# Four interleaved attention layers on one core: earlier statistics and weight requests, later query factors

## The chip, the cores and the metric

The kernel runs on one core of a Trainium2 chip. The metric is the time of one execution on the device, in microseconds (us). A core has TensorE (PE, matmuls and transposes), VectorE (DVE), ScalarE (ACT), GpSimd (POOL) and SyncE (SP), which here does nothing but issue DMAs.

## The reference

Input x has S = 2048 rows of D = 512; there are H = 32 heads of 16. Four layers run in the order A, B, A, B, each as x + layer(layernorm(x)), both A layers with the same weights, both B layers too.

```python
def A(x):                                   # linear attention, learned feature map
    q, k, v = heads(x @ wqkv)
    pq, pk = q @ w_phi[h], k @ w_phi[h]
    phi = lambda p: concat(softmax(p), softmax(-p))       # 16 -> 32 features
    kv, z = phi(pk).T @ v, sum(phi(pk))
    return heads_back((phi(pq) @ kv) / (phi(pq) @ z + 1e-6)) @ wo

def B(x):                                   # four segments of 512 rows
    q, k, v = heads(x @ wq), heads(x @ wk), heads(x @ wv)
    for s in range(4):
        a_dot = softmax(q_s @ k_s.T / 4 + causal_mask) @ v_s
        a_mem = (elu1(q_s) @ M) / (elu1(q_s) @ z + 1e-6)  # M, z: segments before
        o_s = g * a_mem + (1 - g) * a_dot                 # g = sigmoid(beta)
        M, z = M + elu1(k_s).T @ v_s, z + sum(elu1(k_s))
    return heads_back(o) @ wo
```

## The kernel before

Rows are handled in 16 tiles of 128 rows by 512, in segments of four tiles. Between layers x lies in DRAM. All projections run as three matmuls on a high and a low part of each operand (`mm3`), so each transposed tile is made twice: ACT copies the high part out of PSUM (names `hh`, `oh`, `hi`), and DVE takes the difference as the low part (`hl`, `ol`, `lo`; `columns`, `turn` and `proj` do this). A low part inside `wait(...)` is put off by one slot where its table entry ends in "~".

**Order.** Python generators are interleaved step by step, and that order is written out by hand: `Ordered` wraps DVE, ACT, POOL and SP, and inside stretches with `ordered[0]` each engine keeps the program's order. `strict[0]` does the same for PE. SP issues nearly all DMAs in that order, and its issue of one DMA waits for the DMA eight before it.

**Layer A, pass 1** takes segments in the order `SEGS` = 1, 2, 3, 0. For the first layer `first()` writes the start out strictly: it loads the first rows and the raw weights, folds `w_phi` into the query and key weights, splits them into high and low parts, and makes the first v tiles. After it `norm_T` brings the next segment: four row loads into the pool tag `x` (four buffers), `bn_stats` per tile on DVE (`moments`), the root on ACT, the normalisation on ACT (`normal`), then transposes and high and low parts (`columns`). `prepare()` runs beside pass 1 and splits the weights of the later layers by way of DRAM.

**Layer A, pass 2** has 17 iterations, i = 0 to 16. One iteration transposes the query features `P` of tile i in two halves, applies `scale_q` to tile i+1 (sums `es`, reciprocal and factor `rr` on DVE, one product on POOL), turns the output of tile i-1 (`turn`: `oh`, `ol`), multiplies with `KN` in two halves (`weigh`), makes the differences of tile i+3 on POOL, asks for the queries of tile i+4 (`load_q`), projects tile i-1 with `wo` (`out_proj`), adds the residual row tile (tags `xr` and `ot`) and stores it. It then loads the next residual tile. One iteration has nine steps.

**The crossing into layer B.** The first `A20` = 76 steps of pass 2 run before layer B's `steps`. Into them `opening` is interleaved, one step every three from step 42 on. It calls `start()`, which makes two sets of the tiles Q and K (tag `e8`) and fills fixed rows of them by DMAs: mask rows into Q and K, and then ones into K over part of what the mask DMA wrote. Then it asks for the first four row tiles, makes their statistics, and at last asks for the value weights `bwv` (two halves of 1 MB) and for two tiles of `wqk` (0.5 MB each, `queue_w`).

**Layer B** runs slots k from -31 on; `BEFORE` says which projection, v tile or transposition falls into which slot before the first attention product. `maxima` and `attend` make the attention of 32 blocks m of four heads; `finish` transposes a block's result and `weigh`s it into the sums. From the second segment on, `weigh` multiplies on DVE and adds on POOL.

Names in the profile: line 162 is the wrapper of DVE, ACT, POOL and SP, line 184 `mm`, line 188 `tp` (transposes). The tile names carry the reading: `x` row tiles, `xr` and `ot` residual tiles, `g` the PSUM tiles of all projections and transposes, `e<-mask` and `e<-ones` the DMAs of `start()`.

## Time and profile before

| | |
|---|---|
| three runs, median | 1655.01 us |
| lowest and highest | 1649.2 and 1658.6 us |
| profiled execution, its own time | 1656.99 us |
| its span in the trace | 1655.3 us |
| its mean granted PE clock | 0.967 |
| DMA | 195.76 MB, mean 118 GB/s |

The profile is that of one execution. A row of the timeline gives start and duration in us, the engine, the line, the operation with output and input tiles, and in brackets the engine's idle time before it with what released it. A row of the waits gives engine, line and tile, what was waited for, then total us, number and longest. Several equal instructions in a row are one line with a count; the start is that of the first and the time is the engine's.

### The profile page before, as it was taken

To read this page: it belongs to the slowest core of one execution; us is meant where nothing else is said; L and a number is where in the kernel's file an instruction comes from. 1 tells how busy PE (TensorE), PEld (TensorE's weight loads), DVE (VectorE), ACT (ScalarE), POOL (GpSimd) and SP (SyncE) were. 2 spreads that over 40 slices of the span, in tenths; PEclk is the share of its full clock that TensorE was granted. 3 is DMA by queue.
4 is the path that set the end of the run, shared out by engine and by line. 5 is a ranking of instruction groups with operands and counts; after the bars stand their busy time and mean duration, and the time that the engine had idled before them with its cause. 6 is when DMAs were issued, how large, how long until landed. Compare 5 with 4: busy or idle time off the path is not lost.

```text
span 1655.3 us, 28153 instructions
## 1 busy us (share of the span) xinstructions
PE 1532.1 (93%) x9856; PEld 1094.4 (66%) x9856; DVE 1135.8 (69%) x3286; ACT 786.9 (48%) x1178; POOL 643.3 (39%) x972
## 2 busy tenths in 40 slices
PE   7799995998899999999999999788889999999998
PEld 6687884775566666666568888667655666666554
DVE  4575764376787877888655647536677778777783
ACT  4444333324656556556433333233355655654553
POOL 1366642222444354333222336323134445533422
PEclk9999997899999999999999999898999999999999
DMA  7348135434533533534242111454344445343331
GB/s 284 101 134 266 65 100 175 141 109 116 173 97 97 154 90 107 145 96 125 69 159 64 46 70 39 130 193 123 105 133 122 116 116 134 85 135 92 90 87 49
DMA packets 101124, 195.76 MB, mean 118 GB/s; under 512 B 13560, under 2 KB 27128, under 8 KB 97912
## 3 DMA queue, kind: packets, MB, share of 16 engines
q1 hardware_dynamic: 99832, 193.44, 39.2%
q8 instruction: 79, 1.29, 0.3%
q10 hardware_dynamic: 1152, 0.52, 0.1%
q14 instruction: 61, 0.50, 0.1%
HBM read 101.05 MB, written 39.85 MB: 85 GB/s over the span
## 4 chain that ended last, share of the span: by engine, by line
PE 71%; DVE 16%; issue 4%; ACT 4%; DMA 3%; POOL 2%; SPq 1%; ACTq 0%; DVEq 0%; POOLq 0%
PE g L184 43%; DVE mx L162 8%; PE mx L184 8%; PE lg L184 8%; PE pv L184 6%; PE g L188 6%; DVE mxs L162 2%; POOL P L162 1%; ACT tb L162 1%; ACT P L162 1%; DMA wqk<-wqk 1%; DVE es L162 1%; DVE ta L162 1%; DVE bs L162 1%; SPq L162 1%
## 5 line engine op out<-in xcount | busy, mean ns | idle before, releaser
L162 DVE CUSTOM_DVE_ANT_0 mx<-mx,mask 128x128 f32<-128x128 f32 (+3 forms) x1024 | 510.9, 499 | 185.2 <-PE mx L184 150.7
L162 ACT ACTIVATE P<-lg 128x1024 f32<-128x1024 f32 x320 | 328.8, 1028 | 186.8 <-PE lg L184 176.1
L162 POOL TENSOR_SCALAR_AFFINE_SELECT P<-P 128x256 f32<-128x256 f32 (+1 forms) x448 | 191.3, 442 | 445.5 <-ACT P L162 444.2
L184 PE MATMUL g<-hh,wqk 128*128 128x512 f32 x512 | 183.7, 413 | 16.4 <-DMA wqk<-wqk 15.9
L184 PE MATMUL g<-w,oh 128*128 128x512 f32 x512 | 177.4, 429 | 9.1 <-DVE ol L162 5.7
L184 PE MATMUL lg<-e,e 64*128 64x256 f32 (+2 forms) x1024 | 169.5, 389 | 8.1 <-ACT P L162 5.9
L184 PE MATMUL mx<-e,e 63*128 63x256 f32 (+2 forms) x1024 | 156.9, 363 | 21.4 <-DVE mxs L162 15.6
L184 PE MATMUL pv<-P,v 128*32 128x512 f32 (+3 forms) x2048 | 167.4, 446 | 0.0
L184 PEld LDWEIGHTS lg<-e,e 64*128 64x128 f32 x1024 | 81.7, 185 | 104.5 <-issue 55.1
L184 PE MATMUL g<-w,hh 128*128 128x512 f32 x448 | 146.6, 408 | 3.5 <-ACT tb L162 3.0
L162 DVE DVE_READ_ACCUMULATOR2_ANT mxs<- 128x1 f32 x1024 | 144.9, 141 | 0.0
L184 PEld LDWEIGHTS mx<-e,e 63*128 63x128 f32 x1024 | 83.8, 186 | 70.4 <-DVE mxs L162 49.9
L184 PEld LDWEIGHTS g<-hh,wqk 128*128 128x128 f32 x512 | 98.3, 192 | 38.5 <-issue 16.7
L184 PEld LDWEIGHTS pv<-P,v 128*32 128x32 f32 x2048 | 54.0, 110 | 100.2 <-issue 89.4
L184 PEld LDWEIGHTS g<-w,oh 128*128 128x128 f32 x512 | 94.0, 199 | 35.0 <-DVE ol L162 7.0
L162 POOL TENSOR_SCALAR tb<-tb 128x512 f32<-128x512 f32 x48 | 71.5, 1490 | 108.1 <-ACT tb L162 108.1
L184 PE MATMUL g<-w,ol 128*128 128x512 f32 x256 | 105.2, 412 | 1.1 <-DVE ol L162 1.1
L162 ACT CAST ta<-g 128x512 fp32r<-128x512 f32 x64 | 37.5, 586 | 136.1 <-PE g L184 136.0
L184 PE MATMUL g<-hl,wqk 128*128 128x512 f32 x256 | 101.7, 397 | 0.0
L184 PEld LDWEIGHTS g<-w,hh 128*128 128x128 f32 x448 | 80.6, 190 | 23.1 <-ACT tb L162 5.1
L162 POOL TENSOR_TENSOR P<-P,rr 128x512 f32<-128x512 f32 x32 | 33.9, 1060 | 151.2 <-DVE rr L162 151.2
L162 ACT COPY P<-g 128x512 f32<-128x512 f32 x64 | 34.7, 589 | 116.5 <-PE g L188 116.5
(132 smaller groups left out, 2781.8 us busy)
## 6 DMA issues: line engine op xcount, KB each, us to landing
e<-ta SPq DMA_DIRECT2D x384, 128.0 KB
wqk<-wqk SPq DMA_DIRECT2D x64, 512.0 KB
x<-x SPq DMA_DIRECT2D x48, 256.0 KB
xr<-in SPq DMA_DIRECT2D x28, 256.0 KB
pq<-tb SPq DMA_DIRECT2D x24, 256.0 KB
tb<-pq SPq DMA_DIRECT2D x24, 256.0 KB
x<-xr SPq DMA_DIRECT2D x24, 256.0 KB
xr<-x SPq DMA_DIRECT2D x24, 256.0 KB
```

What stands on the lines that cost most here:

```text
L162: i = f(*a, **k)
L184: return held(nc.tensor.matmul(*a, **k))
L188: return held(nc.tensor.transpose(*a))
```

## The change

- In `first()` the next segment's `norm_T` is created before the v weights are split, so its row loads are asked for there, and it is advanced 3, 2, 3 and 2 steps behind the four v tiles (`NEXT`), with its refinement on POOL. Pass 1 then goes on with what is left of it.
- `opening` begins at step 30 of pass 2, not 42: two `queue_w`, the two halves of `bwv`, one a step, then the rows, then `start()`, then the statistics.
- `start()` writes each Q and K tile's fixed rows once: `ones` has 32 rows, taken from a new column of `bd` (one in rows 15 and 31, zero elsewhere), so that no second DMA goes into K.
- `scale_q` of tile i+1 stands behind `turn`, not behind the transposes; that of the second tile of the last segment stands in pass 1 ahead of KN.
- Four entries of `BEFORE` lose their "~".
- For the last block of all, `weigh` adds on DVE and not on POOL.

```diff
+NEXT = (3, 2, 3, 2)
...
-BEFORE = {-30: "ln0", -29: "ln0", -28: "ln0", -27: "ln0", -25: "q0~", -23: "v0", -21: "k0~", -20: "load", -19: "v1",
-          -18: "n", -17: "v2 n", -16: "n", -15: "n n", -14: "q1~ n", -13: "n", -12: "v3 n", -11: "n", -10: "k1~ n",
+BEFORE = {-30: "ln0", -29: "ln0", -28: "ln0", -27: "ln0", -25: "q0", -23: "v0", -21: "k0", -20: "load", -19: "v1",
+          -18: "n", -17: "v2 n", -16: "n", -15: "n n", -14: "q1 n", -13: "n", -12: "v3 n", -11: "n", -10: "k1 n",
...
-        dve.memset(ones, 1.0)
+        dve.tensor_copy(ones, bd[0:32, 25:26].broadcast_to([32, P]))
...
             for t, k in zip((hi, lo), kept[key]):
                 dma(t, k)
+                yield
...
-    def weigh(out, p, eps, add):
+    def weigh(out, p, eps, add, eng=pool):
...
-        pool.tensor_tensor(out=out, in0=out, in1=t, op=ADD)
+        eng.tensor_tensor(out=out, in0=out, in1=t, op=ADD)
...
             next(kfold)
+            side = norm_T(self.xsrc, SEGS[1], nxt, "e8", slow=True, off=True)
+            next(side)
             for kc in range(NC):
...
                         next(qfold)
+                for _ in range(NEXT[t]):
+                    next(side)
...
-                    side = chain(norm_T(self.xsrc, SEGS[n + 1], hTs, spare), v_tile(hTs, wv, vv, ("g", G)))
+                    side = norm_T(self.xsrc, SEGS[n + 1], hTs, spare)
+                    if first and n == 0:
+                        hTs, side = nxt, ahead
+                    side = chain(side, v_tile(hTs, wv, vv, ("g", G)))
...
                     if t == 6:
+                        scale_q(e[5])
                         KN = self.KN = sp.tile([P, 8, 4, VW], F32, tag="KN", bufs=1, name=nm("KN"))
...
-                        if half == 1 and i + 1 < NT:
-                            scale_q(self.e[i + 1])
                         yield
                 if i > 0:
                     oT = turn([o[:, c * P : (c + 1) * P] for c in range(NC)])
+                    if i + 1 < NT:
+                        scale_q(self.e[i + 1])
...
-                for t in (Q, K):
-                    dma(t[3:P:4].rearrange("p a t -> p (a t)"),
-                        mask[0:32, 0:P].unsqueeze(1).broadcast_to([32, 16, P]))
-                dma(K[63:P:64].rearrange("p a t -> p (a t)"), ones[0:2, :].unsqueeze(1).broadcast_to([2, 16, P]))
+                for t, rows in ((Q, mask[0:32, 0:P]), (K, ones)):
+                    dma(t[3:P:4].rearrange("p a t -> p (a t)"), rows.unsqueeze(1).broadcast_to([32, 16, P]))
...
-                  pt.rearrange("p (q h e) -> p q h e", q=4, h=4), 0.0, s > 0)
+                  pt.rearrange("p (q h e) -> p q h e", q=4, h=4), 0.0, s > 0,
+                  dve if m == 8 * NSEG - 1 else pool)
...
             self.wnext = [(m, c) for _ in range(NSEG) for c in range(NC) for m in range(2)]
-            self.start()
-            self.norm0 = self.norm(0)
-            for _ in range(11):
-                next(self.norm0)
-                yield
-            self.wv = load_w("bwv")
             for _ in range(2):
                 self.queue_w()
+                yield
+            w = []
+            side = bring(w, "bwv")
+            self.wv = w
+            for _ in side:
+                yield
+            self.norm0 = self.norm(0)
+            next(self.norm0)
+            self.start()
+            for _ in range(10):
+                yield
+                next(self.norm0)
...
-            if k >= 42 and k % 3 == 0:
+            if k >= 30 and k % 3 == 0:
```

More of the change, by code (lines that the diff above doesn't have):

```diff
@@ L193, in interleave_kernel @@
     ident = cp.tile([P, P], F32, name="ident")
-    bd = cp.tile([P, 25], F32, name="bd")
+    bd = cp.tile([P, 26], F32, name="bd")
     bdA, bdB = bd[:, 0:8], bd[:, 8:16]
@@ L199, in interleave_kernel @@
     share = cp.tile([P, 8], F32, name="share")
-    ones = cp.tile([4, P], F32, name="ones")
+    ones = cp.tile([32, P], F32, name="ones")
     def constants():
@@ L568, in __init__, with first @@
             self.pqs, self.e, self.raw = {}, {}, {}
-        def first(self, hT, vv):
+        def first(self, hT, vv, nxt):
             ordered[0] = strict[0] = True
@@ L630, in first @@
             floor.update(ends)
-            return wq, wk, wv
+            return wq, wk, wv, side
         def pass1(self, first):
-            hTs, vv = [], []
+            hTs, vv, nxt = [], [], []
             if first:
-                wq, wk, wv = self.first(hTs, vv)
+                wq, wk, wv, ahead = self.first(hTs, vv, nxt)
             else:
@@ L1258 @@
     p = np.arange(P)
-    bd = np.zeros((P, 25), np.float32)
+    bd = np.zeros((P, 26), np.float32)
+    bd[[15, 31], 25] = 1.0
     bd[p, 24] = p % 32 < 16
```

## The prediction

> **What bounds the kernel now.** I read the page's first part first, because it tells which engine can set the time at all.

> ```profile
> span 1655.3 us, 28153 instructions
> PE 1532.1 (93%) x9856; PEld 1094.4 (66%) x9856; DVE 1135.8 (69%) x3286; ACT 786.9 (48%) x1178; POOL 643.3 (39%) x972
> ```

> PE is busy for 1532.1 of 1655.3 us, and the change removes no matmul. So no more than 1655.3 - 1532.1 = 123.2 us of idle time can be won, plus what PE lost by running at a lower clock. Next I read PE's own waits (total, times, longest, in us), because only a wait of PE is worth anything here.

> ```profile
> PE g L184 <- DVE xr L162: 18.5, 2, 9.7
> PE g L184 <- DMA wqk<-wqk: 15.9, 2, 8.1
> PE g L188 <- ACT x L162: 8.1, 1, 8.1
> PE g L184 <- DVE ol L162: 6.8, 6, 1.7
> PE g L188 <- ACT tb L162: 5.6, 2, 2.8
> PE g L188 <- POOL P L162: 3.5, 2, 1.8
> PE g L188 <- POOL tmp L162: 3.2, 2, 2.5
> ```

> These seven rows hold 61.6 us, and each edit aims at one or two of them. I took them one at a time, with the timeline around each. A fast measurement here spreads from 1649.2 to 1658.6 us, so about 0.5% (8 us) is what can be told from no change. The profiled execution took 1656.99 us: its span and 1.7 around it, 1.98 above the median 1655.01. All sums are made against 1656.99, and 1.98 is taken off at the end.

> **Second rows' statistics among the first weights.** The windows give us, PE busy (instructions), granted PE clock, DMA share, GB/s; the rows under them are PE's, SP's and DVE's in the same stretch.

> ```profile
> 41.00:49.00 8.00, 0.26 (x1) 0.77 0.36 148
> 49.00:59.00 10.00, 7.40 (x32) 0.84 0.38 106
> ...
> 37.05 0.62 PE L184 MATMUL g<-w,hh 128*128 128x512 f32 x2
> 49.91 7.21 SPq L162 DMA_DIRECT2D x<-in  x4
> 53.34 0.69 DVE L162 BATCH_NORM_STATS2 bs<-x 128x6 f32<-128x512 f32 x1 [0.86 <-DMA x<-in]
> 55.34 0.68 DVE L162 TENSOR_TENSOR e<-g,e 128x512 fp32r<-128x512 f32 x1
> 56.07 0.66 PE L188 MATMUL g<-ident,x 128*128 128x128 f32 x4 [1.91 <-DVE e L162]
> ```

> Between 41 and 59 PE works 7.66 of 18 us: 10.3 idle, 8.1 of it waiting for ACT to normalise the second rows (the third row of the waits). In the changed order their loads stand ahead of the weight rows that the side stream fetches, their moments run during the first value tiles, and PE finds them normalised. The price is the *third* rows' load. It can be issued only when the first second-row tile has been transposed and its buffer is free, and its statistics stand on DVE ahead of a low part (the e tile) that frees the PSUM tile for PE's next transposes. From the issue at 49.91 to the statistics at 53.34 is 3.4; statistics and low part are 0.69 + 0.68; together 4.8. PE now has ten instructions between, six matmuls (37.05 shows two plus one low product about every 0.7) and four transposes of 0.66: 2.0. So a stall of 2.8 stands where the 1.91 stood, with about 0.5 around it: 3.3. The clock of 0.84 over 7.40 busy us cost 1.2, which comes back. Sum: 10.3 - 3.3 + 1.2 = 8.2; bounds 3 (the loads of rows and weights collide earlier, and a second stall like the first follows) and 10.

> **Rows asked for sooner, masks later (the two crossings from pass 2 into a B layer).** First PE's and DVE's rows, with SP's issues among them:

> ```profile
> 242.00 1.04 PE L188 MATMUL g<-ident,P 128*128 128x128 f32 x8
> 244.12 1.38 SPq L162 DMA_DIRECT2D e<-mask  x2
> 248.15 1.04 PE L188 MATMUL g<-ident,P 128*128 128x128 f32 x8
> 249.97 1.10 PE L184 MATMUL g<-KN,P 128*128 128x68 f32 x8
> 254.98 0.55 SPq L162 DMA_DIRECT2D e<-ones  x1
> 255.58 1.82 SPq L162 DMA_DIRECT2D x<-x  x4
> 258.31 0.69 DVE L162 BATCH_NORM_STATS2 bs<-x 128x6 f32<-128x512 f32 x1 [11.84 <-DMA x<-x]
> 259.87 1.98 PE L184 MATMUL g<-KN,P 128*128 128x68 f32 x8 [8.79 <-DVE xr L162]
> 267.79 1.03 PE L188 MATMUL g<-ident,P 128*128 128x128 f32 x8
> ...
> 264.00:266.00 2.00, 2.00 (x6) 0.50 0.00 0
> ...
> 1053.94 1.04 PE L188 MATMUL g<-ident,P 128*128 128x128 f32 x8
> 1073.97 1.04 PE L188 MATMUL g<-ident,P 128*128 128x128 f32 x8
> ```

> An iteration of pass 2 lasts 6.15 (242.00 to 248.15). The next lasts 19.64, and the one at 1053.94 20.03: 13.5 and 13.9 are lost. PE names the residual addition on DVE, but DVE itself had waited 11.84 for the B layer's rows, which SP issued at 255.58 only, because the ones wait for the masks into the same tile and SP issues in order. In the change no ones wait for a mask, and the rows are issued ahead of all four. They stand instead behind two wqk tiles (0.5 MB each), the two halves of bwv (1 MB each) and some 0.75 MB of the iteration's own traffic. These are asked for four opening steps earlier: 12 steps of pass 2, of which an iteration has 9, so 12/9 x 6.15 = 8.2 us before 244.12, from 236 on.

> What rate will they get? The nearest row is the later load of the same weights.

> ```profile
> 281.37 0.91 SPq L162 DMA_DIRECT2D w<-bwv  x2
> 282.78 0.59 ACT L162 CAST hh<-g 128x512 fp32r<-128x512 f32 x1 [0.41 <-PE g L188]
> 283.40 0.69 DVE L162 TENSOR_TENSOR hl<-g,hh 128x512 fp32r<-128x512 f32 x1 [0.17 <-ACT hh L162]
> 290.80 0.77 PE L184 MATMUL g<-hh,wqk 128*128 128x512 f32 x1 [8.06 <-DMA wqk<-wqk]
> 295.35 0.62 PE L184 MATMUL g<-w,hh 128*128 128x512 f32 x2
> ```

> Two bwv halves and one wqk tile, 2.5 MB, land from 281.37 to 290.80; less the 2.7 that a lone row tile needs (255.58 to 258.31), that is some 0.34 to 0.37 MB a us. With 3.75 MB ahead, and the start spread over 8 us, the first row lands between 248 and 252; I take 251.5. PE stops at 251.07 (249.97 + 1.10) for the residual addition, which follows statistics and low part: a stall of about 3.1. The next iteration's residual tile now stands *behind* the masks, which took from 244.12 to past 254.98 to issue through; I put it 3 to 8.5 late, and take 5. So about 8.1 of 13.5 and 13.9 remains, and 5.4 and 5.8 are won, 11.2 together; each may be 2 (the residual lands with the last mask) to 9 (only the rows' stall stays).

> The row at 264 shows the clock at 0.50 after the 8.79 wait. [...]

> **Weights asked for sooner.** In the rows at 282 to 290, PE has transposed the normalised rows by 282.74 (290.80 - 8.06) and then waits 8.06 for wqk, which had been issued behind 2 MB of bwv. With wqk and bwv asked for about 45 us sooner, what stays is the high and low part that the projection also needs: 282.78 + 0.59, then 283.40 + 0.69 = 284.09, a wait of 1.3 each time. The twelve matmuls from 290.80 to 295.35 took 4.55, where three take 0.7 at full clock (37.05), so 2.8: 1.75 come back each time. Sum: 15.9 - 2 x 1.3 + 2 x 1.75 = 16.8; below 13 only if another load takes wqk's place.

> **Query factors behind the low part; less put off behind maxima.** The chain of one quiet iteration:

> ```profile
> 224.33 1.21 DVE L162 TENSOR_REDUCE es<-P 128x64 f32<-128x1024 f32 x1
> 225.17 0.60 ACT L162 CAST oh<-g 128x512 fp32r<-128x512 f32 x1
> 226.07 0.69 DVE L162 TENSOR_TENSOR ol<-g,oh 128x512 fp32r<-128x512 f32 x1
> 226.30 1.06 POOL L162 TENSOR_TENSOR P<-P,rr 128x512 f32<-128x512 f32 x1 [5.06 <-DVE rr L162]
> 229.68 1.04 PE L188 MATMUL g<-ident,P 128*128 128x128 f32 x8
> ...
> 341.37 0.74 PE L184 MATMUL g<-w,oh 128*128 128x512 f32 x2 [1.70 <-DVE ol L162]
> ```

> Now the sums and the reciprocal stand ahead of the low part; where PE has nothing else, that is the 1.70 at 341.37. Afterwards the low part starts when oh ends, 225.77, and ends at about 226.5; the sums take 1.21 and end at 227.7. From their end now, 225.54, to POOL's start at 226.30 the factors and the hand-over take 0.76, so POOL starts at 228.4 and its 1.06 ends at 229.5. PE's transposes come at 229.68: the cover is down to 0.2 us, and I cost it at nothing. The four low parts that lose their "~" stand ahead of a slot's maxima, not behind them. Of ol's 6.8 (some of it inside the crossings) and the 5.6 on ACT's tb I take 3.5; bounds 0 and 6.

> The factors of the second pass-2 tile, now ahead of the KN product in pass 1, take most of the 3.5 of POOL's P: 2.5 (0 to 3.5). The last addition on DVE follows the product there without a hand-over from engine to engine, in place of POOL's: 1.0 of the 3.2 on tmp (0 to 1.5).

> **The sum.** 8.2 + 11.2 + 16.8 + 3.5 + 2.5 + 1.0 = 43.2. From 1656.99 that is 1613.8; less 1.98, 1611.8, so 1612.

> **Rivals.** *The crossing stalls only move.* The rows stand behind 3.75 MB. If that moves at the rate of the masks' stretch and not of the lone weights, nothing is won there.

> ```profile
> 246.00:248.00 2.00, 2.00 (x11) 1.00 0.79 167
> ```

> At 167 GB/s, 3.75 MB take 22 us from 236 on, to 258, as late as now. Against it: those 167 are small mask pieces, which no longer stand in front. [...] Then the 11.2 vanish: 1623.

> *Everything favourable:* crossings keep 4.5 each and start and low parts give their upper bounds: 43.2 + 7 + 1.8 + 2.5 + 1 = 55.5, so 1600.

> *Slower: the factor chain becomes pass 2's period.* The new order oh, low part, sums, factors, POOL, transposes has 0.2 us to spare. If POOL serves its two differences (about the 1.06 of the row at 226.30 each) ahead of the multiplication, each iteration is longer by 2.1 - 0.2 = 1.9. Over 15 iterations in two layers that is 57 us, against 43: about 1669. It decides from 43.2 / 30 = 1.4 us an iteration; below 1 us it only takes a part. Against it: in the changed order the multiplication stands ahead of the differences in each iteration, and POOL waited 5.06 for the factors.

> That the change does not do what it says I leave out: the moves stand in the changed order of the instructions.

> **Chances.** Forecast 0.70, moved stalls 0.13, all favourable 0.08, slower 0.06, and 0.03 for gains that cancel within 8 us. The range reaches from 1597 (the favourable case less 3 of spread) to 1633 (moved stalls, with the start at its bound of 3 and low parts at 0: 1612 + 11.2 + 5.2 + 3.5 = 1632). Faster by over 0.5% 0.90, within 0.5% 0.04, slower 0.06.

> **What would show it.** Right: among PE's waits no wqk; no 8.1 on ACT x, but one of about 3 us on DVE near 40; in the crossings one stall near 3 and one near 5, the second for a residual tile behind the masks; no wait for POOL's P at the start of pass 2; an iteration of 6.15. Wrong: a longer iteration with PE waiting for POOL's P, rows that land as late as now, or wqk still named.

## The result, and the profile after

The changed kernel takes 1603.32 us in the median of six runs (1594.59 to 1606.38), the kernel before 1655.79 beside it; the ratio is 0.968, with a 95% interval from 0.965 to 0.971. The forecast was 1612, range 1597 to 1633. The profiled execution took 1601.45 us, 55.5 less than that of the kernel before (1656.99), where the sum of the forecast was 43.2. The page of the changed kernel begins:

```profile
span 1599.7 us, 28160 instructions
PE 1512.0 (95%) x9856; PEld 1079.1 (67%) x9856; DVE 1135.5 (71%) x3282; ACT 786.5 (49%) x1178; POOL 642.9 (40%) x976
```

The number of matmuls is the same, 9856, and yet PE is busy for 20.1 us less (1532.1 to 1512.0). Its idle time fell by 35.5 (123.2 to 87.7). So more than a third of the gain is no wait at all but the same work in less time. That is PE's clock: the time for which PE works at half clock falls from 76.8 to 31.3 us in the two traces, and half of that difference, 22.7, is what the same work takes less at full clock (measured are 20.1; eight products of 68 columns took 1.10 us at full clock and 1.98 at half in the trace of before, at 249.97 and 259.87). To see where, the span is cut at the same PE instructions in both traces. The columns are the stretch, its length, PE busy (instructions), granted PE clock, DMA share, GB/s. Before, for the first pair of layers:

```profile
0.00:210.84 210.84, 187.25 (x992) 0.98 0.50 169
210.84:242.00 31.16, 29.06 (x186) 0.95 0.26 85
242.00:273.93 31.93, 21.68 (x121) 0.79 0.49 142
273.93:296.00 22.07, 13.68 (x72) 0.77 0.53 191
296.00:370.00 74.00, 67.93 (x357) 0.91 0.44 132
```

And after:

```profile
0.00:205.39 205.39, 187.95 (x992) 0.98 0.52 174
205.39:232.82 27.43, 27.07 (x185) 1.00 0.36 109
232.82:257.50 24.68, 21.38 (x121) 0.86 0.87 296
257.50:273.11 15.61, 12.38 (x72) 1.00 0.21 69
273.11:340.40 67.29, 62.66 (x358) 1.00 0.48 145
```

The rows are pass 1, the first five iterations of pass 2, the crossing, B's first projection with its weights, and B's opening. The clock column says it: where the kernel before ran at 0.77 to 0.95, the changed one runs at 1.00, except in the crossing (0.86). With the same cuts in the second pair, the gain by stage, split into PE's idle and busy time, is:

| stage | forecast | measured, both pairs | of it idle | of it busy |
|---|---|---|---|---|
| pass 1 with the start | 8.2 | 5.5 | 6.2 | -0.7 |
| pass 2, first iterations | 2.5 | 7.3 | 3.5 | 3.8 |
| crossings | 11.2 | 14.2 | 13.9 | 0.3 |
| weights | 16.8 | 12.5 | 10.1 | 2.4 |
| B's opening (low parts) | 3.5 | 12.6 | 2.3 | 10.3 |
| the rest, with the ends | 1.0 | 3.5 | -0.6 | 4.1 |
| sum | 43.2 | 55.6 | 35.5 | 20.1 |

PE's waits in the changed kernel, those that answer to the rows of before, and new ones (lines 185 and 189 are now `mm` and `tp`, line 163 the wrapper):

```profile
PE g L185 <- ACT P L163: 6.1, 8, 2.0
PE g L189 <- ACT P L163: 5.6, 11, 2.9
PE g L185 <- DVE xr L163: 4.8, 2, 2.7
PE g L189 <- ACT tb L163: 3.0, 2, 1.5
PE g L189 <- DVE e L163: 2.2, 1, 2.2
PE mx L185 <- DVE P L163: 2.1, 1, 2.1
```

The wait of 15.9 for wqk, the 8.1 on ACT's x and the 3.5 on POOL's P are gone, and xr fell from 18.5 to 4.8. New are waits of 2.0 on ACT's P in both layers, one of 2.9 at the end of the first B layer, and one of 2.1 on DVE's P. The crossing, in rows of SP, DVE and PE:

```profile
235.97 3.22 SPq L163 DMA_DIRECT2D x<-x  x4
243.00 0.69 DVE L163 BATCH_NORM_STATS2 bs<-x 128x6 f32<-128x512 f32 x1 [3.46 <-DMA x<-x]
244.58 1.98 PE L185 MATMUL g<-KN,P 128*128 128x68 f32 x8 [2.05 <-DVE xr L163]
252.47 0.66 PE L189 MATMUL g<-ident,tmp 128*128 128x128 f32 x4 [0.32 <-DVE ot L163]
```

The rows' statistics begin at 243.00, where they began at 258.31; 9 of these 15 us are the lead that PE has by then. The rows are issued 10 us earlier still, but take 7.0 to land in place of 2.7, so that 6 are left. One stall of 2.05 remains, and the residual tile behind the masks, for which I had put 5 us, costs 0.32 here (1.5 to 2.0 in the traces of three experiments that leave the crossing as it is: low parts, second rows, second tile).

### The profile page after: what moved, and what is told of

Its sections match the earlier page's. It is cut to its first block, busy times and chain, and to the rows that moved or that the text cites. A ratio compares the mean times of both kernels' runs of the same rounds, so it can differ in the third digit from the quotient of the medians.

```text
span 1599.7 us, 28160 instructions
## 1 busy us (share of the span) xinstructions
PE 1512.0 (95%) x9856; PEld 1079.1 (67%) x9856; DVE 1135.5 (71%) x3282; ACT 786.5 (49%) x1178; POOL 642.9 (40%) x976
## 4 chain that ended last, share of the span: by engine, by line
PE 67%; DVE 17%; ACT 5%; issue 5%; DMA 3%; POOL 2%; SPq 1%; DVEq 0%; ACTq 0%; POOLq 0%
PE g L185 39%; DVE mx L163 9%; PE mx L185 8%; PE lg L185 8%; PE pv L185 6%; PE g L189 6%; ACT P L163 2%; ACT tb L163 2%; DVE mxs L163 2%; POOL P L163 1%; DVE ta L163 1%; DMA x<-x 1%; DVE es L163 1%; DMA xr<-in 1%; ACT x L163 1%
## 5 line engine op out<-in xcount | busy, mean ns | idle before, releaser
L185 PE MATMUL g<-w,oh 128*128 128x512 f32 x512 | 172.7, 420 | 3.6 <-ACT oh L163 2.7
L185 PE MATMUL g<-w,hl 128*128 128x512 f32 x224 | 88.5, 395 | 0.0
```

The source lines that it names most:

```text
L185: return held(nc.tensor.matmul(*a, **k))
```

## What the clock does with a short stall

The rest of the case turns on this, so it comes ahead of the experiments. In the trace's records of the granted clock, every stretch at half clock inside the span begins and ends on a grid of 3.41 us that runs through the whole trace, and whose place against the program is another in each run: the six of the changed kernel last 3.41 or 6.83 us, the seventeen of the kernel before 3.41 to 13.65. On that grid the changed kernel's crossing and its next stall read (stretch, length, PE busy with its instructions, clock, DMA share, GB/s):

```profile
240.30:243.72 3.42, 1.94 (x16) 1.00 1.03 385
243.72:247.13 3.41, 2.55 (x10) 0.50 1.07 261
247.13:250.54 3.41, 3.41 (x9) 0.50 0.97 265
...
257.37:260.78 3.41, 1.73 (x14) 1.00 0.43 131
260.78:264.20 3.42, 3.10 (x22) 1.00 0.30 102
```

The stall of 2.05 is followed by two stretches at 0.50; the stall of 2.00 at 259 by none. The clearest pair is the stall of 2.08 ahead of the key-value products near 86 us, where the code is the same in two kernels. In the changed kernel:

```profile
83.29:86.70 3.41, 2.57 (x17) 1.00 0.98 246
86.70:90.11 3.41, 2.17 (x20) 1.00 0.74 265
90.11:93.53 3.42, 3.42 (x16) 0.50 0.00 0
```

And in the experiment with extra matmuls in the crossing (below), which lie later:

```profile
83.76:87.17 3.41, 1.96 (x14) 1.00 0.96 265
87.17:90.59 3.42, 2.79 (x25) 1.00 0.54 198
90.59:94.00 3.41, 3.41 (x24) 1.00 0.13 44
```

It is the same stall with the grid 0.47 us further on, and the clock falls in one and not in the other. I counted the grid stretches at full clock in the thirteen traces of this case, from the second one of each record on, where the next lies whole inside the span. Of those in which PE was busy for less than half, 63 of 65 were followed by half clock; of those from 0.5 to 0.7, 53 of 182; from 0.7 to 0.8, 5 of 205; above 0.8, none of 5397. In the traces of the kernel before and of the changed one alone these are 13 of 13, 8 of 26, 2 of 35 and none of 801. The busy share isn't all: in 25 of these 182, products of 68 columns (`KN` and the key-value products) filled 0.2 of the stretch or more, and 23 of the 25 were followed by half clock, against 30 of the other 157 (in the two traces alone 5 of 5, against 3 of 21). The two stalls above agree: the stretch at 240.30 was busy for 0.57, with 0.32 of such products, and was followed by half clock; that at 257.37 was busy for 0.51, with none of them and nearly all transposes, and was not. So what PE worked on went with it too; why is open. In these traces a stall of about 2 us cost its length alone (1.9 for one of 1.76, in the experiment on the second tile's factors) or, by where it fell on the grid and by the work around it, 1.7 us (half of 3.41), 3.4 or more on top (6.1 for another of 1.76 there), as far as PE didn't wait behind it for something that came no sooner.

The spread of the runs went with the clock. The six runs of the changed kernel, with their mean granted clock, are 1594.59 (0.993), 1599.53 (0.990), 1601.45 (0.989), 1606.38 (0.986), 1605.63 (0.985) and 1605.19 (0.984): 0.009 of clock is 14 us of 1600, and the times differ by 12. That the place of the grid makes this difference is likely, but only one of the six runs has a trace.

## The experiments

Each changes one part of the changed kernel. Since the kernel before itself ran at 1650 to 1653 on the chips of these runs, and at 1656 on that of the result, medians and ratios can differ by 2 to 9 us in what they say (the changed kernel was not run beside them); where a few us matter, I read the two traces against each other, by the start of the same PE instruction. "Later" means later than in the changed kernel's trace.

**Low parts put off again.**

```diff
-BEFORE = {..., -25: "q0", ..., -21: "k0", ..., -14: "q1 n", ..., -10: "k1 n",
+BEFORE = {..., -25: "q0~", ..., -21: "k0~", ..., -14: "q1~ n", ..., -10: "k1~ n",
```

> The changed kernel with the four entries of BEFORE put off again (q0~, k0~, q1~, k1~); nothing else differs. Clock theory (the gain beyond the forecast is PE's clock: a PE stall of about 2 us costs its own length and one or more stretches of 3.41 us at half clock): the 2.80 us wait on tb comes back in both B layers in place of 1.50, and with it windows at a clock of 0.50 behind it, 10.2 us long as in the kernel before: about 1.3 + 5 for each layer, 12 in all, so 1615. Waits theory (the edit is worth the waits alone that it takes away): 2 x 1.3 = 2.6, so 1606.

Measured: 1608.84 us, ratio 0.977 (0.974 to 0.980). The waits' row and a window behind the stall at 289.51 to 292.31:

```profile
PE g L189 <- ACT tb L163: 5.6, 2, 2.8
...
295.00:300.00 5.00, 5.00 (x19) 0.50 0.15 52
```

The wait is 2.8 again in place of 1.5, and in both layers 10.24 us at half clock stand behind it. Across the stall and what follows PE comes 4.7 later in each layer: 1.3 of it wait, 3.4 clock. The waits theory gave 1.3 for each and falls; the clock theory's 6.3 was somewhat high. The times alone would not tell: the median lies nearer to the 1606 of the waits theory, the ratio (0.977 of 1655.79 is 1617) nearer to the 1615 of the clock theory.

**Query factors ahead of the low part again** (from the second iteration on).

```diff
+                        if half == 1 and 0 < i and i + 1 < NT:
+                            scale_q(self.e[i + 1])
...
                     oT = turn([o[:, c * P : (c + 1) * P] for c in range(NC)])
-                    if i + 1 < NT:
-                        scale_q(self.e[i + 1])
```

> The changed kernel with the query factors of pass 2 from the second iteration on behind the transposes again, ahead of the low part; the factors of the second tile stay in pass 1. Clock theory: the wait of 1.70 on the low part in B's opening comes back with one stretch of 3.41 us at half clock (1.7), and each quiet iteration takes 6.15 in place of 6.04; 1.5 + 1.7 + 14 x 0.11 = 4.7 for each layer, so +9 and 1612. Waits theory: 1.5 + 1.5 for each layer, +6, so 1609. Rival of the prediction (the chain of factors is near to being the period): the iteration gets shorter, not longer, and the time falls below 1600.

Measured: 1609.59 us, ratio 0.975 (0.973 to 0.977). First this experiment's waits and two of its iterations, then the same two of the changed kernel:

```profile
PE g L185 <- DVE ol L163: 6.8, 6, 1.7
...
214.90 1.04 PE L189 MATMUL g<-ident,P 128*128 128x128 f32 x8
221.06 1.04 PE L189 MATMUL g<-ident,P 128*128 128x128 f32 x8
```

```profile
214.71 1.09 PE L189 MATMUL g<-ident,P 128*128 128x128 f32 x8
220.75 1.09 PE L189 MATMUL g<-ident,P 128*128 128x128 f32 x8
```

All six waits on ol are back, 6.8 as before, and an iteration takes 6.16 in place of 6.04. The edit does make iterations shorter, against the rival of the prediction. Of the two waits of 1.69 in B's opening, one was followed by a stretch at half clock and one was not. Times of 1609 and 1612 were expected, and the measured one does not tell the two theories apart.

**The opening in the old order, with the new masks.**

```diff
+            self.start()
+            self.norm0 = self.norm(0)
+            for _ in range(11):
+                next(self.norm0)
+                yield
+            self.wv = load_w("bwv")
             for _ in range(2):
                 self.queue_w()
...
-            if k >= 30 and k % 3 == 0:
+            if k >= 42 and k % 3 == 0:
```

> The changed kernel with the opening of the B layer in the old order and at the old place (masks and ones, rows with their statistics, then bwv, then two wqk, from step 42 on), but with the new masks and ones, none of which waits for another. Order theory (the rows must stand ahead of the masks, and the weights ahead of both): the 8 us wait for wqk is back in both layers (about 6.3 each with its clock) and the rows still land late behind the mask pieces, 4 to 7 of each crossing's 7.1: +21 to +27, so 1624 to 1630. Dependency theory (the crossings were late because the ones waited for the masks): only the wqk wait is back, +12.6, so 1616.

Measured: 1626.16 us, ratio 0.987 (0.984 to 0.991).

```profile
PE g L185 <- DMA wqk<-wqk: 15.2, 2, 7.7
...
PE g L185 <- DVE xr L163: 8.5, 2, 4.5
```

The wait for wqk is back whole. The crossing's stall is 4.5: half of the 8.8 before, and twice the 2.05 after. So the ones that waited for masks made about half of that stall, and the order the other half and all of the wqk wait. The median is in the order theory's range (the ratio says 1635, above it).

**Masks and ones as before, in the new order.**

```diff
-                for t, rows in ((Q, mask[0:32, 0:P]), (K, ones)):
-                    dma(t[3:P:4].rearrange("p a t -> p (a t)"), rows.unsqueeze(1).broadcast_to([32, 16, P]))
+                for t in (Q, K):
+                    dma(t[3:P:4].rearrange("p a t -> p (a t)"),
+                        mask[0:32, 0:P].unsqueeze(1).broadcast_to([32, 16, P]))
+                dma(K[63:P:64].rearrange("p a t -> p (a t)"), ones[0:2, :].unsqueeze(1).broadcast_to([2, 16, P]))
```

> The changed kernel with the old masks and ones (the ones' DMA into K waits for the mask in it), in the new order: weights, rows, then masks and ones. Order theory: the rows stand ahead of the masks, so their stall stays at 2 to 3; but SP is held up behind the two ones until the masks have landed, and with it the next store and residual load: 3 to 6 us more in each crossing, 1609 to 1615. Dependency of no weight (the residual has an iteration of room): 1603 to 1605.

Measured: 1617.32 us, ratio 0.979 (0.976 to 0.982).

```profile
PE g L185 <- DVE ot L163: 12.2, 2, 7.4
```

This is the stall that I had priced at 3 to 8.5: the residual tile behind the masks, 7.35 in the first crossing and 4.85 in the second. It comes up here because SP is held up by ones that wait for masks (in the trace of before SP waits four times for a mask, 15.7 us in all); the change removed that too, and I had not counted on it. The time is above the 1609 to 1615 of the order theory.

**B's weights asked for 12 steps earlier.**

```diff
-            if k >= 30 and k % 3 == 0:
+            if (18 <= k < 30 or k >= 42) and k % 3 == 0:
```

> The changed kernel with the weights of the B layer (two wqk, two halves of bwv) asked for in steps 18 to 27 of pass 2 and not 30 to 39; rows, masks and ones stay at step 42. Queue theory (the rows land late because 3 MB of weights stand ahead of them): the rows land about 3 us after their issue, the stalls of 2.05 and 2.75 on the residual addition go, and with them two stretches of 3.41 us at half clock in each crossing: 5.5 for each, so 1592. Rival (the rows' own landing and the masks set it): the stalls stay above 1.5 and the time is 1601 to 1603.

Measured: 1603.68 us, ratio 0.972 (0.970 to 0.975).

```profile
PE g L189 <- DVE ot L163: 8.4, 3, 4.1
...
PE g L185 <- DVE xr L163: 2.5, 3, 1.2
```

The queue theory was right for the rows: without 3 MB ahead of them the longest stall on xr falls from 2.7 to 1.2. But a new one of 3.15 and 4.08 stands one iteration later, on ot: PE reaches the next residual tile sooner, and in SP's order the masks stand ahead of that. The stall moved, with its clock, and the time did not change; 1592 had been expected if the rows' stall were all.

**Early weights, and the masks one set at a time, later.**

```diff
-            for b in range(NSET):
+        def fill(self):
+            for b in range(1):
...
-            for _ in range(10):
+            for j in range(10):
                 yield
                 next(self.norm0)
+                if j in (4, 7):
+                    self.fill()
...
```

> The changed kernel with B's weights asked for in steps 18 to 27, the rows at 42, and the masks and ones not at 42 but one set at step 57 and one at 66. Queue theory: without masks ahead of it the residual tile of the next iteration lands in time, so that the new stalls of 3.15 and 4.08 us that stood there with early weights go as well, with their stretches at half clock: 2 x (3.15 + 0.5 + 3.4) = 14 at most against the early weights alone (1603.7), 1590 to 1595. Rival (masks delay the first residual tile that follows them wherever they stand): stalls of 3 us on ot remain an iteration or two later, and the time is 1600 to 1604.

Measured: 1603.52 us, ratio 0.971 (0.967 to 0.974).

```profile
PE g L189 <- DVE ot L163: 6.3, 5, 1.5
```

The longest wait on ot is now 1.5 and all five sum to 6.3; PE's idle time is 85.8 in place of 87.7, and 37.5 us of the span run at half clock in place of 35.0. Both theories are half right: the stall is cut, and what is left still meets the grid. No better version came of it.

**Without the second rows' part.**

```diff
-            side = norm_T(self.xsrc, SEGS[1], nxt, "e8", slow=True, off=True)
-            next(side)
...
-                for _ in range(NEXT[t]):
-                    next(side)
```

> The changed kernel without the second rows' part: their loads and statistics come after the first v tiles again, as in the kernel before; all else as changed. Clock theory: the start loses the idle time and the half clock that the forecast counted, but the stall of 2.08 us before the key-value products near 88 us and the 6.83 us at half clock behind it, which take back some 4.7 of the lead, go too: +5.5 and 1609. Waits theory (the lead of 8.6 us that stands at 85 us is the worth of the part): +8 to 9, so 1612.

Measured: 1609.66 us, ratio 0.974 (0.970 to 0.978). The 8.1 on ACT's x is back. Against the changed kernel, PE stands 8.5 later at 80 us, 3.6 at 100 us and 2.9 from 140 to 240 us, in a trace whose first load came 0.4 sooner: the lead is real, and more than half of it is given back, 4.7 of it between 85 and 100 us, at the stall of 2.08 before the key-value products and the half clock behind it, which this kernel does not have. The part is worth about 3.3 in these traces, less than either theory said. The rest of the difference between the traces arises behind 240 us, where the two kernels are the same.

**The second tile's factors in pass 2 again.**

```diff
+                        if half == 1 and i == 0:
+                            scale_q(self.e[1])
...
-                        scale_q(e[5])
```

> The changed kernel with the factors of the second query tile made in pass 2 behind the transposes of the first again, and not in pass 1. Clock theory: the wait of 1.77 us for P comes back in both A layers and one stretch of 3.41 us at half clock with it: 2 x (1.77 + 1.7) = 6.9, so 1610. Waits theory: 3.5, so 1607.

Measured: 1611.67 us, ratio 0.976 (0.972 to 0.980).

```profile
208.71 1.97 PE L189 MATMUL g<-ident,P 128*128 128x128 f32 x8 [1.76 <-POOL P L163]
```

A wait of 1.76 is back in both layers. In the first, 10.24 us at half clock go with it and PE comes 6.1 later across it; in the second the same wait meets no half clock and costs 1.9. One edit, one wait, and two prices. The busy share does not explain this pair: the grid stretch ahead of the half clock was busy for 0.67, most of it products of 68 columns, and that around the second wait, most of it transposes, for only 0.48. That second stretch is one of the two exceptions below a half.

**Extra matmuls in the crossing's stall.**

```diff
+                        if i == 6 and half == 0:
+                            fill = PS("pv", PV)
+                            for _ in range(8):
+                                mm(fill, lhsT=self.wo[0][:, 0, 0:P], rhs=self.wo[0][:, 0, :], start=True, stop=True)
```

> The changed kernel with eight extra matmuls of 0.23 us (128x512, their result read by nobody) that wait for nothing, put into PE's stall in the crossing iteration of each A layer, between the two halves of the product with KN, where PE waits 2.05 and 2.75 us for the residual addition. They take no work away: 3.7 us of matmuls are added. Clock theory: the stall becomes busy time of the same length, PE keeps its full clock, and the 6.83 us at half clock behind each stall go: 2 x 3.4 saved, less 0.3, so 1597. Waits theory (PE's time is its waits): nothing gained, or up to 3.7 lost, so 1603 to 1607.

Measured: 1610.41 us, ratio 0.974 (0.970 to 0.978).

```profile
243.72:247.13 3.41, 3.18 (x18) 1.00 0.89 290
...
254.43:257.84 3.41, 1.41 (x12) 1.00 0.44 154
257.84:261.26 3.42, 3.42 (x16) 0.50 0.23 77
...
242.76 0.73 PE L185 MATMUL g<-w,oh 128*128 128x512 f32 x2 [1.02 <-DVE ol L163]
248.59 0.66 PE L189 MATMUL g<-ident,tmp 128*128 128x128 f32 x4 [1.32 <-DVE ot L163]
```

The half clock behind the first crossing is gone, as the clock theory said, but the expected 1597 is missed, and the time is above both ranges. At full clock PE only comes sooner to the next inputs and waits 1.02 and 1.32 for them, where the changed kernel waited 0.32: it is 4.1 us ahead of the changed kernel before the crossing's stall (a lead from the start of the trace) and 3.9 after it, so nothing was won there. And the next stall of 2.00 now lies whole in one stretch of the grid, and the clock falls there.

**Extra matmuls in several stalls.**

```diff
+    def idle(n, w):
+        t = PS("pv", PV)
+        for _ in range(n):
+            held(nc.tensor.matmul(t, lhsT=w[0][:, 0, 0:P], rhs=w[0][:, 0, :], start=True, stop=True))
...
+                        if first and n == 0 and i == 2:
+                            idle(9, wv)
...
+                    if i == 8:
+                        idle(8, self.wo)
...
+                        if i == 6 and half == 0:
+                            idle(9, self.wo)
...
+            if table_end is LAST:
+                idle(12, self.wo)
```

> The changed kernel with extra matmuls of 0.23 us, read by nobody, in five stalls of PE: nine before the third transposes of the start (stall 2.16), nine in the crossing iteration and eight two iterations later in each A layer (2.05 and 2.75; 2.00 twice), twelve before the last turn of the first B layer (2.86). The stall ahead of the first segment's last key-value products stays unfilled. Window theory (in ten traces PE's clock is halved for 3.41 us after a stretch of 3.41 us, on a fixed grid, in which PE was busy for less than 0.5, sometimes from 0.5 to 0.7, and never above 0.8): 37.1 us at half clock become 10 to 15, so about 11 to 13 us less busy time for the same work, 1591 to 1594 against 1603. Waits theory: the same time as the changed kernel, 1603 to 1606, with the extra matmuls' overhang on top.

Measured: 1607.74 us, ratio 0.973 (0.970 to 0.976). In the profiled execution 41.0 us of the span run at half clock, not 10 to 15. The filled stalls keep their clock, but the stalls on ot, tb and DVE's P that were not filled lost it in this trace. The 55 extra matmuls make 55 x 0.23 = 12.7 us of work and took only 8.9 of idle time. So as a remedy this fails; that the busy share of a stretch decides was read from the counts above, and no run moved the clock at will.

**The last addition on POOL again**.

```diff
-                  dve if m == 8 * NSEG - 1 else pool)
+                  pool)
```

> The changed kernel with the last addition of the last block on POOL again. If the 1.5 us by which the changed kernel's lead grows in the last 40 us are this hand-over, the end comes 1.0 to 1.5 us later behind the last block; if not, nothing changes there.

Measured: 1603.52 us in one run. First this kernel at the end of the first B layer, then the changed kernel:

```profile
826.38 0.65 PE L189 MATMUL g<-ident,tmp 128*128 128x128 f32 x4 [2.48 <-POOL tmp L163]
```

```profile
825.62 1.21 DVE L163 TENSOR_REDUCE es<-P 128x64 f32<-128x1024 f32 x1
826.81 0.42 DVE L163 TENSOR_TENSOR tmp<-tmp,wt 128x256 f32<-128x256 f32 x1
827.38 1.08 PE L189 MATMUL g<-ident,tmp 128*128 128x128 f32 x4 [2.86 <-ACT P L163]
```

With DVE the wait is 2.86, with POOL 2.48: DVE's addition stands behind a reduction of 1.21 in its own queue and ends at 827.23 (the profile names ACT for this wait). The edit costs 0.4 there, and in these two traces 1.2 of clock behind it, since the changed kernel then runs 6.83 us at half clock and this one 3.41. At the end of the second B layer, whose last block has the edit too, both kernels wait alike; the 1.5 that the changed kernel gains there is a stretch at half clock that the kernel before had at 1625.7.

## Why the prediction was right, and where not

The time lies in the range, the direction holds, and the waits went for the reasons given. The step that failed is one term of the sum that runs through all parts: the clock. I counted 1.2 us at the start and 2 x 1.75 behind wqk, 4.7 in all; measured are 20.1. What I had read were the long waits of 8 us. That stalls of 1.7 and 2.8 us were followed by half clock stood in the same trace (10.24 us at 0.50 from 318.38 on, behind the wait of 2.80 on tb, and 3.41 from 342.27 on, behind that of 1.70), and I priced those waits at their length. The other side of the sum, idle time, was 38.5 forecast and 35.5 measured. That the total still fell inside the range is in part luck. Start and weights came out 7.0 below their terms and the others 19.4 above, and the range's lower end was set by the crossings, the start and the low parts' waits; no rival had this clock in it.

- *Start:* 5.5 for 8.2, or 6.2 when the first load is left out, which came 0.7 later in this trace than in that of before. The stall of the third rows' load came out at 2.16, for 2.8. What I did not name is what the lead meets later: the key-value products reach DVE's P 2.08 too early, and the half clock behind that takes more. The experiment without the part shows it.
- *Crossings:* 14.2 for 11.2. The rows landed as worked out (statistics at 243.0, 7 us after the issue), with a stall of 2.05 and 2.75, for 3.1. The residual's 5 us did not come; the experiment with the old ones shows that it was their wait for masks that would have made it. The stall was followed by 6.83 us at half clock in both, which the sum does not have, though the row at 264 shows the clock at 0.50 behind a stall in the same place; the experiment that filled it won next to nothing in the crossing itself.
- *Weights:* 12.5 for 16.8. The wait for wqk went whole. In its stretch a wait of 2.00 is new in each layer:

```profile
259.06 1.52 ACT L163 ACTIVATE x<-x,st 128x512 f32<-128x512 f32 x2 [4.36 <-POOL st L163]
260.49 1.05 ACT L163 COPY P<-g 128x512 f32<-128x512 f32 x2
261.10 1.11 PE L185 MATMUL g<-KN,P 128*128 128x68 f32 x8 [2.00 <-ACT P L163]
```

  PE now comes to these iterations sooner than the rows' statistics do, and ACT normalises two row tiles ahead of the copy that PE needs. I had written that what stays is the high and low part that the projection needs, and overlooked this.
- *Low parts and less put off:* 12.6 for 3.5, of which 2.3 idle and 10.3 clock. With the wait of 2.80 cut to 1.51 and that of 1.70 gone, the 10.24 and 3.41 us at half clock behind them in each layer went; the first experiment shows 3.4 of clock for each layer from the "~" alone.
- *Second tile's factors:* 7.3 for 2.5 (with the shorter iterations, 0.12 us each against those of the second experiment, which I had left at 6.15). The two waits went, and their clock.
- *Last addition:* a loss of 0.4 and more where I put a gain of 1.0; I had left out what else stands in DVE's queue.
- *Rivals:* the moved stall did not come true in the change. A stall that only moves came up in the experiment with early weights, though there it was a residual tile behind the masks and not the rows behind the weights. The slower case stayed away, but close by: POOL's product ends at 226.73 and PE's transposes start at 226.79, 0.06 us where I had worked out 0.2.

```profile
225.67 1.06 POOL L163 TENSOR_TENSOR P<-P,rr 128x512 f32<-128x512 f32 x1 [2.94 <-DVE rr L163]
```

What stays open: how much of each stage's clock gain a single trace shows by luck of the grid. The time at half clock fell from 109 to 35 us of the span between the two profiled executions; the traces of the experiments lie at 37 to 65, those without one of the edits among them, all far below the 109. But the split by stage is that of one trace each.

## What to carry to other kernels

Read the granted clock behind every stall of the bounding engine, not only the longest: here a stall of 1.76 us cost 6.1 in one layer and 1.9 in the other, and a third of the gain (20.1 of 55.6) was clock. Filling such a stall with useless work kept the clock in the first crossing (1.00 at 243.72, for 0.50), but was worth nothing, since the next input came no sooner. When a request is moved forward in an engine's order of issue, ask which other request it now stands ahead of and who waits for that: the rows behind 3 MB of weights took 7.0 us to land, in place of 2.7; asking still sooner for the weights only moved the stall on by one iteration. And the spread between runs of one kernel need not be noise without a cause: look at whether it goes with the granted clock (here 0.993 at 1594.59 and 0.984 at 1605.19).
